# Output stores on ScalarE's queue, and another bounce tile for the sums of banks, in a fused attention and feed-forward kernel

## The chip, the cores and the metric

The kernel runs on one core of a Trainium2 chip. The metric is the device time of one execution in microseconds; of the kernel before there are three runs (609.57, 611.8 and 612.82 us, median 611.8) and one profiled execution (613.76 us, of which the profile covers a span of 611.9 us). The engines named below are TensorE (PE, with its weight loads as PEld), VectorE (DVE), ScalarE (ACT), GpSimd (POOL) and SyncE (SP), which does nothing but issue DMAs here. A queue name with a q at its end (SPq, ACTq) is the engine's instruction queue, where DMAs are issued.

## The reference

Decayed linear attention over blocks of 64 positions, then two matrix products with a leaky ReLU between:

```python
# q, k, v: (4, 8, 768, 64); lam: (8,);  w_in: (512, 2048); w_out: (2048, 512)
for b in range(nb):                       # 12 blocks of 64 positions
    intra = einsum('bhic,bhjc->bhij', qb, kb) * Dmask
    intra = einsum('bhij,bhjd->bhid', intra, vb)
    inter = einsum('bhid,bhde->bhie', qb * lam_pow, kv_state)
    out[:, :, sl] = intra + inter
    kv_state = lam_block * kv_state + einsum('bhsd,bhse->bhde', kb * rev_pow, vb)
x = out.transpose(0, 2, 1, 3).reshape(3072, 512)
h = x @ w_in
g = maximum(0.01 * h, h)
return g @ w_out                          # (3072, 512)
```

The products of the second part are done in three partial products each: an operand is split into a head `h` (ScalarE scales it by a little less than one into the reduced float32 form that TensorE takes), a rest `l` and a middle `m` (one VectorE pass each). A "conversion" below is this: one ScalarE instruction (L811, the head) and two VectorE passes (L814, L818), after which three matmuls per tile, over h, l and m, use the result.

## The kernel before

The 3072 tokens are six groups of 512, and the groups go in three pairs (`pr` 0 to 2, `gi` 0 and 1 within a pair). Until about 360 us the kernel does the attention and, woven into it, the first product with the leaky ReLU (`up`), whose results go to DRAM. After that it is in the stage that matters here, the product with `w_out`.

This stage is a list of units. `s(t, u)` is a product of a Strassen-like scheme (kinds 1 to 7, each in two halves u), `n(p, gi)` a plain product over one slice p of the 2048 columns. Each unit loads 512 KB from DRAM into a slot (`go`, L808, on SP), converts it (L811, L814, L818), and TensorE multiplies (L834). There are five slots used in turn, so a unit takes the slot that the unit five places earlier used, and its load waits until TensorE is done with that one. Kind 4 also loads a second operand into the tile `w32` (L825) and subtracts (L826) before it converts.

The results are summed in eight PSUM banks, in pairs named X, Z, Y and V. X and Z are the tiles `psc` and `po`, Y is `b10` and `b2`, V is `b11` and `pt`; the profile shows the three `b` banks alike as `b`. In the second and third pairs the order is: the last four units of the pair before (its `gi` = 1) mixed with `s(1,*)` and `s(6,*)`; a copy of X into Z and of Z into Y (`copy_banks`, L918, two ScalarE copies each); `s(5,*)`; Y += V (`add_banks`); `s(7,*)`; V += Z; then `s(3,0)`, `n(4,0)`, `s(2,0)`, `n(5,0)`, `s(3,1)`, `s(2,1)`, `n(6,0)`, `s(4,0)`, `s(4,1)`, `n(7,0)`. `add_banks` copies a bank to SBUF with ScalarE (L923) and adds it with VectorE (L924), bank by bank. The SBUF tile of this bounce is a piece of `gs`, which is also the tile `otile` that outputs are collected in.

With a group's last unit each finished bank is transposed from PSUM into `otile` by VectorE (`turn_out`, L902), and the output is stored from there (`store_out`, L911): four DMAs for each half m of a group's tokens, each from 32 partitions. A group's stores are so eight DMAs of 128 KB; the last group's are sixteen of 64 KB, since there two banks are stored as soon as they are ready, and the last bank is done in two halves of 256 columns.

What runs when is decided by a planner (`Plan`) when the program is built. Each operation is added with an engine, an estimated time, the keys it reads and writes, and a rank (place in the list plus an offset). `emit` simulates the engines: it always takes the operation that can start earliest, and among those that can start at the same time the one with the lowest rank. The order so found is fixed in each engine's program; at run time each engine goes through its own in order and waits on semaphores. "DMA" is SP. Conversions have the offset -LEAD (-8.0); copies and sums of banks, transposes and stores have -1.5. A store of four DMAs counts as one SP operation of 1.6 us.

Of the kernel before, what the change touches and what calls it, by code (L numbers as in the profile page):

```python
# [15 lines left out]
ALU = mybir.AluOpType  # L16
# [20 lines left out]
class Plan:  # L37
# [23 lines left out]
    def add(self, eng, us, fn, reads=(), writes=(), rank=0.0):  # L61

        n, deps = len(self.ops), set()
        for k in reads:
            w, r = self.last.setdefault(k, [None, []])
            if w is not None:
                deps.add(w)
            r.append(n)
        for k in writes:
            w, r = self.last.setdefault(k, [None, []])  # L70
            if w is not None:
                deps.add(w)
            deps.update(r)
            self.last[k] = [n, []]
        deps.discard(n)
        ways = {eng: us} if isinstance(eng, str) else dict(zip(eng, us))
        if self.slack:
            self.more[n] = self.slack
        if self.chain is not None:
            self.chains[self.chain].append(n)  # L80
        self.ops.append((ways, fn, deps, (self.rank + rank, n), set(writes)))
# [81 lines left out]
def kernel(  # L163
# [10 lines left out]
    nc = tc.nc  # L174
    P = 128
# [24 lines left out]
    LEAD = 8.0  # L200
# [3 lines left out]
    C4 = P // 4  # L204
# [8 lines left out]
    def sb(shape, name, dt=F32):  # L213
        return pool.tile(shape, dt, name=name, tag=name)
# [17 lines left out]
    w32 = sb([P, 2, d_model], "w32")  # L232
    w32f = w32.rearrange("p h n -> p (h n)")
    gst = sb([P, 2, 2, T], "gs")
    gs = [gst[:, i] for i in range(2)]
    WO = [dram.tile([P, 2 * d_model], F32, name=f"wo{p}", tag=f"wo{p}") for p in range(NP)]
    HT = T // 2
# [42 lines left out]
    add = plan.add  # L280
# [496 lines left out]
    acc = {"X": flat[:2], "Z": flat[2:], "Y": [b1[0], b2], "V": [b1[1], bank["pt"]]}  # L777
    ACC = {"X": ["X0", "X1"], "Z": ["Z0", "Z1"], "Y": ["b10", "b2"], "V": ["b11", "pt"]}
# [13 lines left out]
    def unit(src, keys, f=1, less=None):  # L792

        nonlocal n_ring
        j = slots[n_ring] if n_ring < len(slots) else RING[(n_ring - len(slots)) % NR]
        first, n_ring = j not in slots[:n_ring], n_ring + 1

        def wr(z):
            return [f"r{z}{j}"] + ([f"x{z}{j // 2}{cc}" for cc in range(GC)] if first and j < 4 else [])

        def m_slot():
            return ring[j][2].bitcast(F32)

        def g():
            return m_slot() if less is None else w32f

        def go():
            nc.sync.dma_start(out=m_slot().rearrange("p (f t) -> p f t", f=f), in_=src)  # L808

        def head():  # L810
            nc.scalar.activation(out=ring[j][0], in_=g(), func=AF.Copy, bias=0.0, scale=NEAR)  # L811

        def low():
            nc.vector.scalar_tensor_tensor(ring[j][1], g(), 1.0, ring[j][0].bitcast(F32), op0=ALU.mult, op1=ALU.subtract)  # L814

        def middle():
            h, l, m = ring[j]
            nc.vector.scalar_tensor_tensor(m, l.bitcast(F32), -S, h.bitcast(F32), op0=ALU.mult, op1=ALU.add)  # L818

        kg = [f"rm{j}"]  # L820
        add("DMA", 1.5, go, keys, wr("m"))
        if less is not None:
            x, k = less
            kg = ["w320", "w321"]
            add("DMA", 1.5, lambda: nc.sync.dma_start(out=w32f, in_=x), k, kg)  # L825
            add("DVE", 1.25, lambda: nc.vector.tensor_tensor(w32f, w32f, m_slot(), op=ALU.subtract), [f"rm{j}"], kg)  # L826
        add("ACT", 1.05, head, kg, wr("h"))
        add("DVE", 1.25, low, kg + [f"rh{j}"], wr("l"))
        add("DVE", 1.25, middle, [f"rh{j}", f"rl{j}"], [f"rm{j}"])
        return j  # L830

    def product(dst, j, col, lhs, first=False, n=T):
        for z in range(3):
            nc.tensor.matmul(dst, lhsT=lhs(z), rhs=ring[j][z][:, col:col + n], start=first and z == 0, stop=z == 2,  # L834
                             skip_group_check=True)
# [25 lines left out]
    def plain(pr, p, gi, lead, last=False, banks=None):  # L861

        g = 2 * pr + gi
        here = plan.rank
        plan.rank -= lead
        d = G[pr][p].rearrange("p (f h t) -> p f h t", f=2, h=2)[:, :, gi, :]
        j = unit(d, [x for x in plan.last if x[0] == "G" and x[1] in (str(2 * pr), str(2 * pr + 1)) and x[2:4] == f"{p}{gi}"], 2)
        plan.rank = here
        reads = [f"r{z}{j}" for z in "hlm"] + [f"w{z}{p}" for z in "hlm"]

        def go(fs, cs, lo=0, n=T):
            for f in fs:
                for c in cs:
                    d, i = BANKS[gi][c]
                    product(acc[d][i][:, lo:lo + n], j, f * T + lo,
                            lambda z, f=f, c=c: W[p][z][:, f * 2 * NQ + c * P:f * 2 * NQ + (c + 1) * P], first=pr == p == f == 0, n=n)

        if not last:
            add("PE", 0.227 * 24, lambda: go((0, 1), range(4)), reads, [ACC[d][i] for d, i in BANKS[gi]])
            return  # L880
        end = pr == NG // 2 - 1 and gi == 1
        for i, c in enumerate(banks):
            d, b = BANKS[gi][c]
            parts_ = 2 if end and i == 3 else 1
            for half in range(parts_):
                k = ACC[d][b] + (f"half{half}" if parts_ > 1 else "")
                n = T // parts_
                add("PE", 0.227 * 6 * (1.0 if parts_ == 1 else 0.53), lambda c=c, half=half, n=n: go((0, 1), (c,), half * n, n),
                    reads + ([ACC[d][b]] if parts_ > 1 else []), [k])
                turn_out(c, acc[d][b], [ACC[d][b], k], half * n, n)  # L890
                if i == 3 or end and i == 1:
                    cs = sorted(banks[:2] if end and i == 1 else banks[2:] if end else banks)
                    for m in ([half] if parts_ > 1 else range(2)):
                        store_out(pr, gi, m, cs)

    otile = gst.rearrange("p x f (b c j) -> p (x f b) c j", c=4, j=C4)

    def turn_out(c, b, keys, lo, n):
        nonlocal n_o
        n_o += 1  # L900
        o = otile[:, lo // C4:(lo + n) // C4, c, :]
        add("DVE", 0.1 + 0.6 * n / T, lambda: nc.vector.transpose(out=o, in_=b[:, lo:lo + n].rearrange("p (b i) -> p b i", i=C4)), keys,  # L902
            [f"o{c}{m}" for m in range(lo // HT, (lo + n) // HT)] + (["gs0", "gs1"] if n_o <= 4 else []), rank=-1.5)

    def store_out(pr, gi, m, cs):
        t0, n, w = (2 * pr + m) * T + gi * HT, HT // C4, len(cs) * C4

        def store():
            for a in range(4):
                c0 = a * P + cs[0] * C4  # L910
                nc.sync.dma_start(out=out[t0:t0 + HT, c0:c0 + w].rearrange("(b i) j -> i b j", i=C4),  # L911
                                  in_=otile[a * C4:(a + 1) * C4, m * n:(m + 1) * n, cs[0]:cs[-1] + 1, :].rearrange("i b c j -> i b (c j)"))

        add("DMA", 1.6, store, [f"o{c}{m}" for c in cs], [], rank=-1.5)

    def copy_banks(d, s):
        for i in range(2):
            add("ACT", 0.6, lambda i=i: nc.scalar.copy(acc[d][i], acc[s][i]), [ACC[s][i]], [ACC[d][i]], rank=-1.5)  # L918

    def add_banks(d, s):  # L920
        for i in range(2):
            y, key = gs[i][:, 0, :], [f"o{c}{i}" for c in range(4)]
            add("ACT", 0.6, lambda i=i, y=y: nc.scalar.copy(y, acc[s][i]), [ACC[s][i]], key, rank=-1.5)  # L923
            add("DVE", 0.72, lambda i=i, y=y: nc.vector.tensor_tensor(acc[d][i], acc[d][i], y, op=ALU.add), key, [ACC[d][i]], rank=-1.5)  # L924

    seq = [("a", 0), ("a", 1), ("a", 2), ("a", 3), ("wi", 1), ("b", 4), ("r", 4), ("up", 0, 1), ("wi", 0), ("r", 5),
# [26 lines left out]
    for pr in range(NG // 2):  # L953
# [11 lines left out]
        else:  # L965
            i = seq.index(("up", NG - 1, NP - 1))
# [73 lines left out]
```

## Time and profile before

| | |
|---|---|
| median of three runs | 611.8 us |
| profiled execution | 613.76 us |
| its span | 611.9 us |
| PE busy from 330 to 600 us, by stretches | all but 1.31 us |
| DVE / ACT busy over the span | 387.4 / 290.4 us |
| SP's queue | all DMAs of the kernel but one |
| output stores | 56 DMAs at L911, from 417.7 to 609.5 us |
| end of the last matmul, of the last store's landing, of the span | 603.5, 610.8, 611.9 us |

A row of a timeline has its start, its duration, the engine with the line of the kernel, the operation with out<-in tiles, and in brackets how long the engine was idle before and whom it waited for. A row of the chain of work has start, duration, and engine or DMA. The duration of a DMA row on SPq is the time that its issue took, not the transfer; "x8" there is a run of eight issues put together. Ends of matmuls are modelled, so distances between starts say more than their durations.

### The profile page before, as it was taken

The numbers are of one execution on the slowest core, as the hardware profiler recorded it, in microseconds if no ns is written. First come the engines' busy times: TensorE is split into PE (matmuls) and PEld (weight loads), VectorE is DVE, ScalarE is ACT, GpSimd is POOL, SyncE is SP. The second block draws the span as 40 slices with busy tenths as digits, with TensorE's granted clock in tenths as the row PEclk, the third lists the DMA queues.
The fourth block names the chain that finished last, engine by engine and source line by source line (L and its number), as shares of the span: only waits on it lengthen the run. The fifth ranks groups of instructions, "written<-read, shape, count | busy, mean of one in ns | idle before, by whom it ended". The sixth has DMA issues, their size and how long they took to land.

```text
span 611.9 us, 13190 instructions
## 1 busy us (share of the span) xinstructions
PE 591.6 (97%) x5340; PEld 488.7 (80%) x5340; DVE 387.4 (63%) x534; ACT 290.4 (47%) x458; POOL 85.9 (14%) x90
## 2 busy tenths in 40 slices
PE   7899999999989999999999999999999999999994
PEld 6688888888868877888888888888887888878883
DVE  4899764335436327426589849975688695778831
ACT  4678974445545545565576743432334223251300
POOL 1564422114214003203100000000000000000000
PEclk9899999999989999999999999999999999999998
DMA  9899776767889887999889735436465465474433
GB/s 217 212 261 254 228 193 145 171 151 204 196 218 264 216 220 218 235 235 260 265 256 333 233 113 197 170 123 185 139 182 195 152 193 176 155 225 140 158 80 69
DMA packets 190188, 119.88 MB, mean 196 GB/s; under 512 B 128944, under 2 KB 168112, under 8 KB 190128
## 3 DMA queue, kind: packets, MB, share of 16 engines
q1 hardware_dynamic: 189984, 119.05, 68.8%
q8 instruction: 42, 0.69, 0.5%
q14 instruction: 18, 0.15, 0.1%
q10 hardware_dynamic: 144, 0.00, 0.0%
HBM read 79.17 MB, written 39.85 MB: 194 GB/s over the span
## 4 chain that ended last, share of the span: by engine, by line
PE 84%; DMA 4%; SPq 4%; DVE 3%; ACT 2%; issue 1%; DVEq 0%; ACTq 0%
PE b L709 40%; PE b L834 11%; PE psc L834 11%; PE po L834 10%; PE po L321 4%; PE psc L321 4%; PE pt L834 4%; SPq L382 2%; SPq L911 2%; DMA att<-in_v_dram 1%; DMA raws<-in_moe_w_out_dram 1%; DVE xl L814 1%; PE pt L411 1%; DMA xm<-g 1%; DMA raws<-g 1%
## 5 line engine op out<-in xcount | busy, mean ns | idle before, releaser
L709 PE MATMUL b<-xm,wm 128*128 128x512 f32 (+2 forms) x392 | 103.9, 392 | 2.4 <-ACT b L727 2.4
L709 PE MATMUL b<-xh,wh 128*128 128x512 f32 (+2 forms) x392 | 103.5, 387 | 2.3 <-ACT gs L732 1.5
L709 PE MATMUL b<-xl,wl 128*128 128x512 f32 (+2 forms) x392 | 104.4, 390 | 0.0
L709 PEld LDWEIGHTS b<-xh,wh 128*128 128x128 f32 x392 | 72.8, 188 | 18.2 <-ACT gs L732 2.4
L811 ACT ACTIVATE xh<-xm 128x1024 fp32r<-128x1024 f32 x45 | 47.7, 1060 | 81.8 <-DMA xm<-g 50.9
L709 PEld LDWEIGHTS b<-xm,wm 128*128 128x128 f32 x392 | 71.4, 188 | 17.8 <-ACT b L727 3.2
L709 PEld LDWEIGHTS b<-xl,wl 128*128 128x128 f32 x392 | 72.8, 188 | 15.1 <-DVE wl L614 0.3
L732 ACT ACTIVATE gs<-b 128x512 f32<-128x512 f32 (+2 forms) x97 | 56.9, 591 | 50.6 <-PE b L709 37.4
L727 ACT ACTIVATE b<-b 128x512 f32<-128x512 f32 (+2 forms) x97 | 56.1, 581 | 52.2 <-PE b L709 52.0
L814 DVE SCALAR_TENSOR_TENSOR xl<-xm,xh 128x1024 fp32r<-128x1024 f32 x45 | 54.8, 1217 | 28.3 <-ACT xh L811 22.1
L818 DVE SCALAR_TENSOR_TENSOR xm<-xl,xh 128x1024 fp32r<-128x1024 f32 x48 | 58.7, 1225 | 3.5
L470 POOL TENSOR_TENSOR att<-att 128x256 f32<-128x256 f32 x40 | 34.1, 853 | 53.9 <-DVE att L467 53.9
L602 DVE TENSOR_SCALAR w<-w 128x512 int32<-128x512 int32 x32 | 17.6, 550 | 36.9 <-ACT w L596 36.8
L431 POOL TENSOR_TENSOR att<-att 128x512 f32<-128x512 f32 (+1 forms) x20 | 25.2, 1261 | 102.0 <-DVE att L391 53.9
L460 DVE TENSOR_TENSOR att<-psc,att 128x512 f32<-128x512 f32 x24 | 16.5, 689 | 31.3 <-PE psc L321 31.2
L321 PEld LDWEIGHTS po<-att 64*64 64x64 f32 x1472 | 28.3, 140 | 9.1 <-issue 6.0
L321 PE MATMUL po<-att 64*64 64x64 f32 x1472 | 34.1, 228 | 0.6 <-ACT att L499 0.3
L427 POOL TENSOR_TENSOR att<-att 128x512 f32<-128x512 f32 (+1 forms) x23 | 26.7, 1161 | 53.7 <-DMA att<-in_k_dram 35.9
L603 DVE CUSTOM_DVE_ANT_0 w<-w,lows 128x1024 uint16<-128x1024 uint16 x32 | 26.3, 821 | 12.6 <-ACT lows L600 11.4
L834 PE MATMUL b<-xl,wl 128*128 128x512 f32 (+1 forms) x86 | 33.0, 384 | 0.0
L834 PE MATMUL b<-xm,wm 128*128 128x512 f32 (+1 forms) x86 | 33.0, 384 | 0.0
L834 PE MATMUL b<-xh,wh 128*128 128x512 f32 (+1 forms) x86 | 33.0, 384 | 0.0
(149 smaller groups left out, 1011.2 us busy)
## 6 DMA issues: line engine op xcount, KB each, us to landing
g<-gs SPq DMA_DIRECT2D x31, 512.0 KB, 4.1
xm<-g SPq DMA_DIRECT2D x25, 512.0 KB, 4.7
xm<-b SPq DMA_DIRECT2D x23, 512.0 KB, 3.8
raws<-in_moe_w_in_dram SPq DMA_DIRECT2D x16, 512.0 KB, 5.5
raws<-in_moe_w_out_dram SPq DMA_DIRECT2D x16, 512.0 KB, 5.0
b<-gs SPq DMA_DIRECT2D x16, 512.0 KB, 3.7
att<-in_k_dram SPq DMA_DIRECT2D x48, 128.0 KB, 4.0
att<-in_v_dram SPq DMA_DIRECT2D x24, 256.0 KB, 4.5
```

The lines of the kernel that those rows point to most:

```text
L321: nc.tensor.matmul(dst[HALF[cols]], lhsT=lhsT[HALF[rows]], rhs=rhs[HALF[rows]], start=start, stop=True, skip_group_check=True)
L427: lambda e="POOL": ENG[e].tensor_tensor(kr[nr], kr[nr], _bc(pow_k, 3, D)[nr], op=ALU.mult), ["fk"], [f"k{i}"])
L431: add(eng, us, lambda: e.tensor_tensor(o, x, _bc(pow_q, 2, 2)[:, :, m, :], op=ALU.mult), ["fq", dep], [f"qsT{i}"])
L470: add("POOL", 0.7, lambda new=new, j=j: nc.gpsimd.tensor_tensor(state[(j + 1) % 4], new, _bc(lam_c, 2, D), op=ALU.mult), [f"st{j % 4}", "f ...
L603: add("DVE", 1.0, lambda: nc.vector.tensor_tensor(d, d, low, op=ALU.add), [kl], [key])
L709: nc.tensor.matmul(dst, lhsT=w[z][:, kk * 2 * P + f * P:kk * 2 * P + (f + 1) * P], rhs=x[z][:, kk, toks], start=start and kk == 0, stop=kk ...
L727: add("ACT", ns, lambda b=b: nc.scalar.activation(out=b, in_=b, func=AF.Copy, bias=0.0, scale=S + 1.0), [], [kb], rank=-1.5)
L732: add("ACT", t, lambda o=o, x=s_: nc.scalar.activation(out=o, in_=x, func=AF.Prelu, bias=0.0, scale=(1.0 + 1.0 / S) / (WS * U), alpha=0.01 ...
L811: nc.scalar.activation(out=ring[j][0], in_=g(), func=AF.Copy, bias=0.0, scale=NEAR)
L814: nc.vector.scalar_tensor_tensor(ring[j][1], g(), 1.0, ring[j][0].bitcast(F32), op0=ALU.mult, op1=ALU.subtract)
L818: nc.vector.scalar_tensor_tensor(m, l.bitcast(F32), -S, h.bitcast(F32), op0=ALU.mult, op1=ALU.add)
L834: nc.tensor.matmul(dst, lhsT=lhs(z), rhs=ring[j][z][:, col:col + n], start=first and z == 0, stop=z == 2, skip_group_check=True)
```

## The change

Three things are changed. The stores are added to the plan one DMA at a time, at 0.5 us: those of all groups but the last go to ScalarE, with rank offset 6.0 in place of -1.5; those of the last group go to ScalarE and SP in turns, with -1.5. The bounce of `add_banks` lies in the tile `w32`, with its keys, instead of in `gs` with the keys of the output tile. Copies and sums of banks have the rank offset -LEAD, like conversions.

```diff
-                        store_out(pr, gi, m, cs)
+                        store_out(pr, gi, m, cs, end)
...
-    def store_out(pr, gi, m, cs):
+    def store_out(pr, gi, m, cs, last):
         t0, n, w = (2 * pr + m) * T + gi * HT, HT // C4, len(cs) * C4
 
-        def store():
-            for a in range(4):
-                c0 = a * P + cs[0] * C4
-                nc.sync.dma_start(out=out[t0:t0 + HT, c0:c0 + w].rearrange("(b i) j -> i b j", i=C4),
-                                  in_=otile[a * C4:(a + 1) * C4, m * n:(m + 1) * n, cs[0]:cs[-1] + 1, :].rearrange("i b c j -> i b (c j)"))
-
-        add("DMA", 1.6, store, [f"o{c}{m}" for c in cs], [], rank=-1.5)
+        def store(a, q):
+            c0 = a * P + cs[0] * C4
+            q.dma_start(out=out[t0:t0 + HT, c0:c0 + w].rearrange("(b i) j -> i b j", i=C4),
+                        in_=otile[a * C4:(a + 1) * C4, m * n:(m + 1) * n, cs[0]:cs[-1] + 1, :].rearrange("i b c j -> i b (c j)"))
+
+        for a in range(4):
+            e = "DMA" if last and (a + m) % 2 else "ACT"
+            add(e, 0.5, lambda a=a, e=e: store(a, nc.scalar if e == "ACT" else nc.sync), [f"o{c}{m}" for c in cs], [], rank=-1.5 if last else 6.0)
 
     def copy_banks(d, s):
         for i in range(2):
-            add("ACT", 0.6, lambda i=i: nc.scalar.copy(acc[d][i], acc[s][i]), [ACC[s][i]], [ACC[d][i]], rank=-1.5)
+            add("ACT", 0.6, lambda i=i: nc.scalar.copy(acc[d][i], acc[s][i]), [ACC[s][i]], [ACC[d][i]], rank=-LEAD)
 
     def add_banks(d, s):
         for i in range(2):
-            y, key = gs[i][:, 0, :], [f"o{c}{i}" for c in range(4)]
-            add("ACT", 0.6, lambda i=i, y=y: nc.scalar.copy(y, acc[s][i]), [ACC[s][i]], key, rank=-1.5)
-            add("DVE", 0.72, lambda i=i, y=y: nc.vector.tensor_tensor(acc[d][i], acc[d][i], y, op=ALU.add), key, [ACC[d][i]], rank=-1.5)
+            y, key = w32[:, i, :], [f"w32{i}"]
+            add("ACT", 0.6, lambda i=i, y=y: nc.scalar.copy(y, acc[s][i]), [ACC[s][i]], key, rank=-LEAD)
+            add("DVE", 0.72, lambda i=i, y=y: nc.vector.tensor_tensor(acc[d][i], acc[d][i], y, op=ALU.add), key, [ACC[d][i]], rank=-LEAD)
```

## The prediction

> **What bounds the kernel now.** I read the shares first, then the matmuls of the last stage by stretches, then the two places where they pause, then the tail.
>
> ```profile
> PE 591.6 (97%) x5340; PEld 488.7 (80%) x5340; DVE 387.4 (63%) x534; ACT 290.4 (47%) x458; POOL 85.9 (14%) x90
> 410.00:599.00 189.00, 187.69 (x826) 154.53 (x826) 1.00 0.52 162
> 600.00:612.00 12.00, 3.53 (x22) 2.98 (x20) 0.75 0.41 87
> ```
>
> TensorE is busy for 97% of the span. All output stores lie after 410 us. From there to 599 us (second row: window, length, PE busy, weight loads, clock, DMA share, GB/s) the matmuls lack 1.3 us out of 189, so an edit to this stage can win almost nothing except in those pauses and in the last 8.4 us, where PE has stopped (third row). The pauses:
>
> ```profile
> 462.65 0.39 PE L834 MATMUL psc<-xl,wl 128*128 128x512 f32 x1
> 463.52 0.50 PE L834 MATMUL psc<-xm,wm 128*128 128x512 f32 x1 [0.48 <-DVE xm L818]
> 545.17 0.50 PE L834 MATMUL psc<-raws,wl 128*128 128x512 f32 x1
> 546.50 0.50 PE L834 MATMUL psc<-raws,wm 128*128 128x512 f32 x1 [0.83 <-DVE raws L818]
> ```
>
> A matmul takes 187.69 / 826 = 0.227 us in this stage. Here the steps between starts are 0.87 and 1.33 us: 0.64 and 1.10 us too long, 1.74 us together. The chain of work that ended last says why:
>
> ```profile
> 454.80 0.48 SPq L911
> 455.39 4.35 DMA xm<-g
> 459.82 1.07 ACT xh L811
> 460.91 1.24 DVE xl L814
> 462.24 1.24 DVE xm L818
> ...
> 535.12 1.82 SPq L911
> 538.57 4.14 DMA raws<-g
> ```
>
> Both pauses are the first product of `n(4,0)`, the first plain product of the second and of the third pair of groups. Its data were loaded late because SP was issuing eight output stores, as SP's queue shows, and the buffer had been free for some time:
>
> ```profile
> 450.31 4.97 SPq L911 DMA_DIRECT2D out_dram<-gs  x8
> 455.39 0.52 SPq L808 DMA_DIRECT2D xm<-g  x1
> 532.76 5.71 SPq L911 DMA_DIRECT2D out_dram<-gs  x8
> 538.57 0.52 SPq L808 DMA_DIRECT2D raws<-g  x1
> 601.52 7.96 SPq L911 DMA_DIRECT2D out_dram<-gs  x16
> 451.31 0.39 PE L834 MATMUL pt<-xm,wm 128*128 128x512 f32 x1
> 533.76 0.39 PE L834 MATMUL pt<-raws,wm 128*128 128x512 f32 x1
> ```
>
> With five buffers in turn, `n(4,0)` takes the one that `s(5,0)` used; its last matmuls are the last two rows, starting at 451.31 and 533.76, so by the ends of these rows it is free at 451.70 and 534.15. The loads went out at 455.39 and 538.57: 3.7 and 4.4 us later, with the stores between. The fifth row is the tail, sixteen stores one after another on SP.
>
> **The change part by part.**
>
> *Stores of all groups but the last, SP to ScalarE.* 40 of the 56 DMAs of L911 leave SP. SP's next loads can go when their buffer is free: 451.7 instead of 455.4, and 534.15 instead of 538.6. They now share the DMA engines with the stores, so I don't take the landings of 4.35 and 4.14 us but the longest of this stretch:
>
> ```profile
> DMA to landing us min/median/max: 3.3/3.8/5.4
> ```
>
> 451.7 + 5.4 = 457.1; then head 1.07 and two DVE passes of 1.24, with 0.1 of gaps: 460.8. The third matmul is due at 462.88. In the next pair 534.15 + 5.4 + 3.65 = 543.2, due at 545.4 less the 0.64 won before, 544.76. Both pauses go, by 2.1 and 1.6 us. What is late next is then that same unit, through DVE (below). Gain 1.74 us; bounds 0 (the loads win nothing) and 2.1 (the three matmuls that show 0.50 us instead of 0.39 beside a pause become short too, 0.33 us more).
>
> *What it costs ScalarE.* ScalarE's program in the first of the two places:
>
> ```profile
> 450.32 0.57 ACT L918 COPY b<-po 128x512 f32<-128x512 f32 x1 [0.73 <-DVE gs L902]
> 450.80 1.06 ACT L811 ACTIVATE xh<-xm 128x1024 fp32r<-128x1024 f32 x1
> 452.97 1.06 ACT L811 ACTIVATE xh<-xm 128x1024 fp32r<-128x1024 f32 x1 [1.11 <-DMA xm<-b]
> 455.29 0.59 ACT L923 COPY gs<-b 128x512 f32<-128x512 f32 x1 [1.25 <-DMA out_dram<-gs]
> 457.21 0.59 ACT L923 COPY gs<-pt 128x512 f32<-128x512 f32 x1 [1.33 <-PE po L834]
> 459.82 1.06 ACT L811 ACTIVATE xh<-xm 128x1024 fp32r<-128x1024 f32 x1 [2.02 <-DMA xm<-g]
> ...
> L911 SPq DMA_DIRECT2D out_dram<-gs x56: 316/468/1822, 417.7 to 609.0; - x56
> ```
>
> A store waits only for transposes that are over when it becomes ready; but as the queue is in order, heads and copies stand behind it while it issues. The head of `n(4,0)` must start by 462.88 - 1.07 - 2.48 - 0.1 = 459.2. From 450.3 that is 8.9 us, less a copy (0.57), two heads (2.12) and two bounces (1.18): 5.0 us are free for eight stores, 0.63 us each. At the tail's pace, 7.96 / 16 = 0.50 us with the gap between issues, they need 4.0 (the median issue of the last row is 0.468). So they are hidden, at 0 us, by ScalarE's waits for loads. Bounds: 0, and the eight stores at 0.71 us each (5.71 / 8): 0.7 us late. Rank 6.0 lets heads and copies that are ready in the plan go first, so I take 0. In the other three groups PE pauses nowhere near the stores (1.3 us is all that is idle up to 599), and what covers them is again ScalarE's waiting for loads; 0.
>
> *Bounce in w32 instead of gs.* The bounce no longer waits for the old stores to have read `gs` (the 1.25 us before 455.29). No pause of PE hung on it, so this wins 0. In return the w32 load of `s(4,0)`, fetched far ahead until now, waits on SP for the second sum, with the loads of `s(2,1)` and later queued behind it:
>
> ```profile
> L825 SPq DMA_DIRECT2D w<-b x4: 320/330/872, 399.3 to 563.6; - x4
> 473.24 0.69 DVE L924 TENSOR_TENSOR b<-b,gs 128x512 f32<-128x512 f32 x1
> 471.59 0.32 SPq L808 DMA_DIRECT2D xm<-b  x1
> 476.91 1.22 DVE L826 TENSOR_TENSOR w<-w,xm 128x1024 f32<-128x1024 f32 x1
> ```
>
> The load that went at 399.3 now goes after the sums, at about 463 us by their new rank, and lands, again at the longest 5.4 us, at 468.4. The subtraction that reads it ran at 476.91, because its other operand was only asked for at 471.59. Cover of 3 us or more; cost 0. Even with the sum left at 473.24 it would be about 479, and DVE's work after that would shift by 2 us: the upper bound.
>
> *Sums ahead of conversions.* The two additions into V ran from 473.24, behind conversions; with rank -8 they run as soon as the copies are there, near 461. That puts 2 x 0.69 = 1.4 us in front of the conversions of `n(4,0)` if both are ready together: 460.8 + 1.4 = 462.2 against 462.88, and 543.2 + 1.4 = 544.6 against 544.76. Just covered, so 0; if landing or stores take a little longer it costs up to 1.4 us per place, but that can't exceed the pause that is there now by much. This is the thin part of the sum.
>
> *The tail.* Here the durations lie open:
>
> ```profile
> 600.78 0.72 DVE L902 STREAM_TRANSPOSE gs<-pt 128x512 f32<-128x512 f32 x1 [0.65 <-PE pt L834]
> 603.57 0.78 DVE L902 STREAM_TRANSPOSE gs<-b 128x256 f32<-128x256 f32 x2 [0.71 <-PE b L834]
> 604.00:605.00 1.00, 0.00 (x0) 0.00 (x0) 0.35 (x2) 0.00 (x0) 0.00 (x0) 1.00 0.59 128
> L1035 SPq EVENT_SEMAPHORE  x8: 17/28/28, 610.8 to 611.9; - x8
> out_dram<-gs SPq DMA_DIRECT2D x16, 64.0 KB, 1.8
> ```
>
> The data of the last eight stores are there at 604.0 and 604.35, but SP, at 0.50 us per store, is with the first eight until 605.5 and starts the last at 609.0; 1.8 us later (last row: bytes of one store, median us to landing) it has landed, 610.8, and 1.1 us of closing follow. With two queues in turn: four each from 601.52, free at 603.5; two each at 604.0 (to 605.0); two each at 605.0, the last starting at 605.5. That is 3.5 us earlier. The DMA engines move 128 GB/s at a share of 0.59, so at full share about 217 GB/s (an estimate from this row): the last eight, 8 x 64 KB = 0.52 MB, need 2.4 us from about 604.6, which ends at 607.0 and some queueing. I charge 0.3 us for it: gain 3.2 us. Bounds: 3.5, and 0 if the two queues can't issue at once. The nearest row for that is the opening, the only place where both issue together:
>
> ```profile
> 0.73 0.43 ACTq L268 DMA_DIRECT2D att<-in_lam_dram  x1
> 0.74 0.46 SPq L346 DMA_DIRECT2D att<-in_k_dram  x1
> ```
>
> They overlap whole and neither is longer than usual, so I take the value for parallel issue. Against it stands the Trainium skill, page "Perfetto Trace Analysis", section "DMA Instruction — HWDGE (DVE, Sync)": descriptors are made in one block that the sequencers share, each locking it for itself while it generates. By that rule alone the tail would win nothing and the sum would be 1.74 us; the overlapped pair does not agree with a lock over the whole issue.
>
> **Sum.** 1.74 + 3.2 = 4.9 us. The profiled execution took 613.76 us (span 611.9 and 1.9 around it), 2.0 above the median of the runs shown, 611.8. So 608.8 in such an execution, and 611.8 - 4.9 = 606.9 as a median.
>
> **Rivals.**
>
> *The queues take turns.* ScalarE's and SP's issues serialise. For it: issues in the crowded stretch were already stretched to 1.82 us on one queue; against it: the opening pair. Loads still get in between stores, so the pauses go: 611.8 - 1.74 = 610.1. The page named above speaks for this one.
>
> *The pauses stay, in another form.* The sums in front on DVE and the stores on ScalarE make `n(4,0)` as late as SP did. For it: the 0.2 us of slack worked out above; against it: the load gains 3.7 and 4.4 us. Only the tail wins: 611.8 - 3.2 = 608.6.
>
> *Slower: ScalarE is held by its stores.* Where the DMA engines are full, an issue waits; on SP that only delays loads, on ScalarE it stops heads and bounces at 450 and 533 us. Free are 0.63 us per store. At 1.2 us each (between the mean of 0.71 and the longest of 1.82), 8 x 0.57 = 4.6 us late, in two places 9.1; less the tail 3.2: 611.8 + 5.9 = 617.7. It decides from (3.1 + 3.2) / 16 + 0.63 = 1.0 us per store. Against it: the mean was 0.62 and 0.71 there, and heads that are ready go first.
>
> **How the numbers follow.** Forecast 0.55 (its own range 605.9 to 608.3: tail 2.8 to 3.5, pauses 0.7 to 2.1, a few tenths of spread between runs), queues in turn 0.14, pauses stay 0.18, ScalarE held 0.09, others 0.04. The range runs from 605.6 to 610.4: it reaches down to both gains at their upper bound (611.8 - 5.6 = 606.2) with some spread, up past the case of queues in turn, and leaves out the held ScalarE and the rest. Half a per cent, about what can be told from no change, is 3.06 us: under 608.74 is faster. Faster: 0.95 of the forecast, half of "pauses stay", 0.01 of the others: 0.62. Slower: 0.09 + 0.01. The rest, 0.28, is the same.
>
> **What would show it.** Right: no store in SP's queue until the last set; `n(4,0)` loaded within half a microsecond of its buffer's release; no idle step above 0.3 us in its matmuls; the last sixteen stores on two queues within 4.2 us, and a span that ends about 5 us after the last matmul instead of 8.4. Wrong: stores on ScalarE of a microsecond and more with heads waiting behind them; issues on the two queues that never overlap or double in length; sums standing between the head and the passes of `n(4,0)`; a new idle step of PE at `s(4,0)` after a w32 load that came late.

## The result, and the profile after

The changed kernel takes 607.94 us as the median of 13 runs (606.0 to 610.33), the kernel before, in 13 runs beside them, 612.43 us (609.57 to 616.61). The ratio is 0.9925, with a 95% interval of 0.9908 to 0.9943: 4.5 us faster. The forecast was 606.9 us and a gain of 4.9 us. The profiled execution took 606.94 us, its span is 605.2 us.

The spans of the two profiled executions differ by 6.7 us, more than the medians. About 2 us of that lie ahead of the first output, where nothing was changed; that part of the kernel moves by as much from run to run (its end, the first L902, lies between 410.6 and 414.6 us in the fourteen traces of this document). So the comparison is best made from a mark inside the trace. The timelines have one on each side of the stage: the first transpose of an output (L902) and the last matmul. First the kernel before, then the changed one:

```profile
413.66 1.31 DVE L902 STREAM_TRANSPOSE gs<-psc 128x512 f32<-128x512 f32 x2 [0.53 <-PE psc L834]
603.25 0.28 PE L834 MATMUL b<-xm,wm 128*128 128x256 f32 x1
```

```profile
411.62 1.31 DVE L902 STREAM_TRANSPOSE gs<-psc 128x512 f32<-128x512 f32 x2 [0.23 <-PE psc L834]
599.05 0.28 PE L834 MATMUL b<-xm,wm 128*128 128x256 f32 x1
```

From the start of the first row to the end of the second it is 603.53 - 413.66 = 189.87 us before and 599.33 - 411.62 = 187.71 us after: 2.16 us gained in the stage. From the end of the last matmul to the end of the span it is 8.37 us before and 605.2 - 599.33 = 5.87 us after: 2.50 us gained in the tail. The sum, 4.7 us, is the gain of the medians within their spread.

**The stage.** The stretch that lacked 1.31 us of matmuls, in the view by stretches of the changed kernel (L834 alone; window, length, PE busy, weight loads, clock, DMA share, GB/s):

```profile
410.00:599.00 189.00, 189.00 (x840) 156.69 (x840) 1.00 0.54 165
```

TensorE no longer pauses. The timeline around the two first products of `n(4,0)` says why; SPq and ACTq rows are issues of DMAs:

```profile
448.29 0.90 ACTq L910 DMA_DIRECT2D out_dram<-gs  x2
448.76 1.06 ACT L811 ACTIVATE xh<-xm 128x1024 fp32r<-128x1024 f32 x1
449.22 1.45 ACTq L910 DMA_DIRECT2D out_dram<-gs  x2
449.28 0.39 PE L834 MATMUL pt<-xm,wm 128*128 128x512 f32 x1
449.70 0.52 SPq L808 DMA_DIRECT2D xm<-g  x1
454.92 0.32 ACTq L910 DMA_DIRECT2D out_dram<-gs  x1
455.29 1.06 ACT L811 ACTIVATE xh<-xm 128x1024 fp32r<-128x1024 f32 x1 [2.20 <-DMA xm<-g]
455.32 1.67 ACTq L910 DMA_DIRECT2D out_dram<-gs  x3
457.71 1.23 DVE L818 SCALAR_TENSOR_TENSOR xm<-xl,xh 128x1024 fp32r<-128x1024 f32 x1
458.86 0.69 DVE L925 TENSOR_TENSOR b<-b,w 128x512 f32<-128x512 f32 x1
460.84 0.39 PE L834 MATMUL psc<-xm,wm 128*128 128x512 f32 x1
460.99 0.38 SPq L825 DMA_DIRECT2D w<-b  x1
...
530.88 0.39 PE L834 MATMUL pt<-raws,wm 128*128 128x512 f32 x1
531.30 0.52 SPq L808 DMA_DIRECT2D raws<-g  x1
```

The load of `n(4,0)` goes out 0.03 us after its buffer comes free (449.28 + 0.39 = 449.67, and 531.27 in the next pair), instead of 3.7 and 4.4 us later. Its data are converted at 457.71 + 1.23 = 458.94 and the third matmul, which needs them, starts at 460.84: 1.9 us of slack. The stores lie in two parts, four ahead of ScalarE's wait for that load and four at its end. That they stop in between has a reason that the prediction did not have. In the trace all DMAs of the program use eight semaphores in turn, and an issue waits until the DMA that used its semaphore before has landed; more than eight are never under way. The fifth store has the semaphore of the load of `n(4,0)`. The load landed at 454.90, the store went at 454.92, and the head, behind it in ScalarE's order, at 455.29: it waited for its load and then 0.3 us for one store.

**The tail.** The same timeline, then the last issues grouped by line (name, count, shortest/median/longest in ns, first and last start), the closing line in the same form, and one microsecond of the tail by stretches:

```profile
597.33 4.43 SPq L910 DMA_DIRECT2D out_dram<-gs  x8
597.33 4.60 ACTq L910 DMA_DIRECT2D out_dram<-gs  x8
```

```profile
L910 SPq DMA_DIRECT2D out_dram<-gs x8: 316/394/474, 597.3 to 601.4; - x8
L910 ACTq DMA_DIRECT2D out_dram<-gs x8: 323/420/497, 597.3 to 601.6; - x8
...
DMA to landing us min/median/max: 2.0/2.5/2.8
```

```profile
L1036 SPq EVENT_SEMAPHORE  x8: 17/28/155, 603.9 to 605.1; - x8
```

```profile
601.00:602.00 1.00, 0.00 (x0) 0.00 (x0) 0.00 (x0) 0.00 (x0) 0.00 (x0) 0.99 0.98 199
```

The two queues issue side by side, at no more per DMA than one queue alone. The last store starts 2.3 us after the last matmul's end (601.6 to 599.33) where it was 5.5 (609.0 to 603.53). But where the DMA engines stood at a share of 0.59 while one queue issued, they are now full, at about 200 GB/s, and the median store takes 2.5 us to land instead of 1.8. The closing begins at 603.9, when SyncE's last store has landed; ScalarE's last, issued at 601.6, lands at 604.1, and the longest wait of the closing (155 ns) is the one for it.

### The profile page after: what moved, and what is told of

Same layout as the page of the kernel before. It is cut to its first block, busy times and chain, and to the rows that moved or that the text cites. A ratio compares the mean times of both kernels' runs of the same rounds, so it can differ in the third digit from the quotient of the medians.

```text
span 605.2 us, 13193 instructions
## 1 busy us (share of the span) xinstructions
PE 589.9 (97%) x5340; PEld 487.4 (81%) x5340; DVE 387.6 (64%) x534; ACT 290.0 (48%) x458; POOL 86.2 (14%) x90
## 3 DMA queue, kind: packets, MB, share of 16 engines
q10 hardware_dynamic: 13200, 5.77, 3.8%
## 4 chain that ended last, share of the span: by engine, by line
PE 89%; DMA 5%; DVE 1%; ACT 1%; SPq 1%; issue 0%; POOL 0%; DVEq 0%; ACTq 0%
PE b L709 38%; PE b L834 13%; PE po L834 13%; PE psc L834 11%; PE pt L834 4%; PE psc L321 4%; PE po L321 4%; DMA b<-gs 2%; DMA raws<-in_moe_w_out_dram 1%; SPq L382 1%; DMA att<-in_v_dram 1%; PE pt L411 1%; DMA att<-in_k_dram 1%; PE po L411 0%; PE b L274 0%
## 5 line engine op out<-in xcount | busy, mean ns | idle before, releaser
L603 DVE CUSTOM_DVE_ANT_0 w<-w,lows 128x1024 uint16<-128x1024 uint16 x32 | 27.8, 868 | 12.4 <-ACT lows L600 11.2
L834 PE MATMUL b<-xl,wl 128*128 128x512 f32 (+1 forms) x86 | 33.0, 384 | 0.0
L834 PE MATMUL b<-xm,wm 128*128 128x512 f32 (+1 forms) x86 | 33.0, 384 | 0.0
L834 PE MATMUL b<-xh,wh 128*128 128x512 f32 (+1 forms) x86 | 33.0, 384 | 0.0
```

The lines of the kernel that those rows point to most:

```text
L603: add("DVE", 1.0, lambda: nc.vector.tensor_tensor(d, d, low, op=ALU.add), [kl], [key])
```

## The experiments

The line numbers of stores and sums shift by a few lines between kernels. "Stage" is the time from the first L902 to the end of the last matmul as above (before 189.87 us, changed kernel 187.71), "tail" what follows to the end of the span (8.37 and 5.87). These two are from one profiled execution each; times are medians, ratios are to the kernel before on the same chip.

| run | stage, us | tail, us | ratio (95%) |
|---|---|---|---|
| changed kernel | 187.71 | 5.87 | 0.9925 (0.9908 to 0.9943) |
| tail_only | 189.93 | 5.61 | 0.9965 (0.9951 to 0.9980) |
| body_only | 206.98 | 8.47 | 1.0306 (1.0285 to 1.0328) |
| bounce_only | 193.52 | 8.36 | 1.0053 (1.0020 to 1.0087) |
| stores_only | 206.60 | 5.69 | 1.0267 (1.0243 to 1.0291) |
| gs_new_ranks | 202.33 | 5.69 | 1.0143 (1.0093 to 1.0194) |
| w32_old_ranks | 198.13 | 5.77 | 1.0099 (1.0067 to 1.0132) |
| sp_late | 187.71 | 5.60 | 0.9923 (0.9899 to 0.9947) |
| twice_on_act | 187.71 | 5.67 | 607.92 us, one run, to 612.78 |
| rank_early | 200.55 | 5.64 | 622.32 us, one run, to 612.78 |
| last_all_act | 187.71 | 8.53 | 609.03 us, one run, to 612.78 |
| two_banks_first | 187.72 | 5.71 | 0.9934 (0.9906 to 0.9962) |
| token_halves | 187.95 | 5.23 | 0.9917 (0.9887 to 0.9947) |

**One part at a time: tail_only, body_only, bounce_only.** The first is the kernel before with only the last set in turns. The diff is against the changed kernel and is cut; tile and ranks are put back in it too:

```diff
+        if not last:
+            add("DMA", 1.6, lambda: [store(a, nc.sync) for a in range(4)], [f"o{c}{m}" for c in cs], [], rank=-1.5)
+            return
         for a in range(4):
             e = "DMA" if last and (a + m) % 2 else "ACT"
...
```

> The kernel before with one part of the change: the last group's sixteen stores go out on ScalarE and SyncE in turns, all else as before. My theory (the tail is won by two queues issuing at once until the transfers bound it; the pauses are another matter): both pauses at the first product of n(4,0) stay, about 0.6 and 1.1 us too long; from the end of the last matmul to the end of the span 5.9 us instead of 8.4; 2.5 us less than the kernel before. Rival (the gain is one of order in the middle of the stage, and the tail only looks shorter): within 0.5 us of the kernel before.

It measured 608.63 us to 610.74: 2.1 us gained. Its tail is that of the changed kernel, its stage that of the kernel before, and the waits of PE between 410 and 599 us (for whom: us, times, longest) all lie in the third pair, at both passes of the unit `n(4,0)`:

```profile
PE psc L834 <- DVE raws L818: 0.8, 1, 0.8
PE psc L834 <- DVE raws L814: 0.4, 1, 0.4
```

By the steps between starts the matmuls there are 0.59 and 1.10 us late. In the second pair the third matmul is 0.26 us late (461.14 to 461.63), too little for this list. The place is the old one, but the sizes, expected at 0.6 and 1.1, move from run to run.

The second run is the kernel before with only the other stores moved to ScalarE, at rank 6.0; the bounce stays in `gs` and the sums at -1.5 (again a cut diff against the changed kernel):

```diff
+        if last:
+            add("DMA", 1.6, lambda: [store(a, nc.sync) for a in range(4)], [f"o{c}{m}" for c in cs], [], rank=-1.5)
+            return
         for a in range(4):
...
+            add(e, 0.5, lambda a=a, e=e: store(a, nc.scalar if e == "ACT" else nc.sync), [f"o{c}{m}" for c in cs], [], rank=-1.5 if last else 6.0)
```

> The kernel before with one part: stores of all groups but the last on ScalarE with rank 6.0, the last group's sixteen on SyncE as before, bounce in gs and old ranks as before. My theory so far (the pauses come only from stores ahead of loads on SyncE): pauses at n(4,0) gone, tail 8.4 us, 1.7 to 2.1 us less. Rival (the bounce in gs now waits for stores that ScalarE issues late): the second copy of Y += V can't start until stores issued at about 456 us have been read, 3 us later; s(3,0) then waits 2 to 2.5 us in each of two places, and the kernel takes 2 to 3 us more than before although n(4,0) is on time.

It measured 629.06 us, 18.3 us slower than before. My theory had no loss at all; the rival had the cause and the place (`s(3,0)`, in two places), but 2 to 3 us for what costs 18. The waits of PE:

```profile
PE b L834 <- DVE b L928: 15.4, 2, 8.4
```

L928 is here the addition of `add_banks`. What it waits for is shown with stores_only, where the same happens.

The third run is the kernel before with only the new bounce tile and the new ranks (the additions and `copy_banks` change theirs likewise):

```diff
-            y, key = gs[i][:, 0, :], [f"o{c}{i}" for c in range(4)]
+            y, key = w32[:, i, :], [f"w32{i}"]
...
-            add("ACT", 0.6, lambda i=i, y=y: nc.scalar.copy(y, acc[s][i]), [ACC[s][i]], key, rank=-1.5)
+            add("ACT", 0.6, lambda i=i, y=y: nc.scalar.copy(y, acc[s][i]), [ACC[s][i]], key, rank=-LEAD)
```

> The kernel before with one part: bounce in w32 and rank -LEAD for copies and sums, all stores on SyncE as before. My theory: n(4,0) is still loaded late; in the program the two sums into V now stand between its two VectorE passes, 1.3 us, so each pause grows by about 1.2 us: 2 us or so slower than before. Rival (order and bounce are what removed the pauses): pauses gone, 1.7 to 2.1 us less.

It measured 614.98 us to 610.74, 0.5% slower. Waits of PE, then VectorE's timeline:

```profile
PE psc L834 <- DVE raws L818: 1.8, 1, 1.8
PE psc L834 <- DVE xm L818: 1.4, 1, 1.4
```

```profile
458.52 1.23 DVE L814 SCALAR_TENSOR_TENSOR xl<-xm,xh 128x1024 fp32r<-128x1024 f32 x1 [3.02 <-ACT xh L811]
459.66 0.70 DVE L924 TENSOR_TENSOR b<-b,w 128x512 f32<-128x512 f32 x1
460.26 0.69 DVE L924 TENSOR_TENSOR pt<-pt,w 128x512 f32<-128x512 f32 x1
460.86 1.22 DVE L818 SCALAR_TENSOR_TENSOR xm<-xl,xh 128x1024 fp32r<-128x1024 f32 x1
```

The two sums stand between the two passes of `n(4,0)`, whose load is still late behind SP's stores, and lengthen its pauses to 3.7 us together (steps between matmul starts of 1.83 and 2.33 us, where 0.227 is usual; the list above shows the idle part). This is the cost that the prediction set an upper bound to (1.4 us per place). In the changed kernel both passes of `n(4,0)` come before the first sum at 458.86. So of the three parts alone one wins 0.35%, one loses 0.5% and one 3.1%, and together they win 0.75%: they can't be added up.

**stores_only.** The changed kernel with bounce and ranks put back (the diff of bounce_only, reversed).

> The changed kernel without its second and third parts: all stores as changed, bounce in gs and ranks as before. If the stores alone make the gain: as the changed kernel, 4.5 us less than before. If the bounce in gs waits for stores issued late on ScalarE: no pause at n(4,0), the tail of the changed kernel (5.9 us), but a wait of 2 to 2.5 us at s(3,0) in two places, so about the time of the kernel before.

It measured 626.3 us, 15.6 us slower than before. ScalarE's timeline, and two rows from the chain of work:

```profile
454.06 0.59 ACT L924 COPY gs<-b 128x512 f32<-128x512 f32 x1 [3.07 <-DMA out_dram<-gs]
454.09 1.04 ACTq L910 DMA_DIRECT2D out_dram<-gs  x2
...
455.19 1.04 ACTq L910 DMA_DIRECT2D out_dram<-gs  x2
459.78 0.59 ACT L924 COPY gs<-pt 128x512 f32<-128x512 f32 x1 [3.55 <-DMA out_dram<-gs]
460.26 1.06 ACT L811 ACTIVATE xh<-xm 128x1024 fp32r<-128x1024 f32 x1
```

```profile
448.73 5.19 DMA out_dram<-gs
...
455.69 4.02 DMA out_dram<-gs
```

The bounce copy overwrites the piece of `gs` that the old stores read, so it waits until they have landed, 5.2 and 4.0 us after their issue beside the early loads. The stores of the second half of the tokens (454.09, 455.19) go out only behind the first copy, so the two waits come one after the other. ScalarE is in order, so the head at 460.26 stands too, and then the sum into Y, which `s(3,0)` needs: PE pauses 7 to 8 us in each of the two pairs. It was not the time of issuing that held ScalarE, but a copy queued on it that waits for a landing.

A pause so long costs more than itself. By stretches of the same kernel, over the pause and behind it (the clock is the third number from the right):

```profile
458.00:464.00 6.00, 0.00 (x0) 0.00 (x0) 3.36 (x4) 2.97 (x4) 0.00 (x0) 0.74 0.37 126
464.00:468.00 4.00, 3.42 (x9) 2.71 (x10) 3.90 (x4) 1.54 (x2) 0.00 (x0) 0.54 0.00 0
```

The granted clock falls to 0.50 at about 460.9, inside the pause, and comes back at about 467.7, some 3 us after the matmuls resume: nine matmuls take from 464.58 to 468.18, 3.6 us, where 9 x 0.227 = 2.0 would do.

**Tile and rank apart: w32_old_ranks and gs_new_ranks.** With the stores on ScalarE, one run has the new tile with the old ranks, the other the old tile with the new ranks.

> The changed kernel with copies and sums back at rank -1.5; the bounce stays in w32. Stores on ScalarE with the bounce in gs cost 15.6 us; this asks which of the other two parts takes that away. My theory: the tile alone, since what was waited for was the stores' reading of gs (landings of 5.19 and 4.02 us in the chain). Then no pause at s(3,0), and within 1 us of the changed kernel. Rival (the copies must also rank ahead of heads): a pause of 1 us or more at s(3,0) or n(4,0), 2 us or more slower than the changed kernel.

> The changed kernel with the bounce back in gs; copies and sums keep rank -LEAD. My theory: a rank can't shorten a wait for a transfer: s(3,0) pauses 6 to 8 us in each of two places, 12 to 16 us slower than the changed kernel. Rival (the rank gets the copies in front of the stores): within 3 us of the changed kernel; the order of the keys makes this impossible for the second copy, whose piece of gs the stores have still to read.

The first measured 618.77 us to 612.58, the second 621.96. My theory that the tile alone is what protects falls, that with `gs` the kernel stays slow holds. w32_old_ranks, waits of PE, then VectorE and ScalarE:

```profile
PE b L834 <- DVE b L925: 6.8, 2, 3.7
```

```profile
452.70 0.59 ACT L924 COPY w<-pt 128x512 f32<-128x512 f32 x1
...
459.99 1.23 DVE L818 SCALAR_TENSOR_TENSOR xm<-xl,xh 128x1024 fp32r<-128x1024 f32 x1
461.13 0.69 DVE L925 TENSOR_TENSOR b<-b,w 128x512 f32<-128x512 f32 x1
```

The copy is done at 453.3, but its sum runs only at 461.13, behind the conversions of two later units, whose loads now arrive early. In the changed kernel both sums into Y are over by 454.7. gs_new_ranks, ScalarE:

```profile
463.24 0.59 ACT L924 COPY gs<-pt 128x512 f32<-128x512 f32 x1 [4.64 <-DMA out_dram<-gs]
```

The new rank does not get this copy past the stores: the four that read its piece of `gs` stand ahead of it. The last of them went at 458.17, after waiting for a load that had its semaphore, and landed 5.0 us later, at 463.17. Stores on ScalarE so need both: the old tile costs 14.6 us of stage, the old ranks 10.4, both together 18.9 (202.33, 198.13 and 206.60 less 187.71).

**Queue or order: sp_late, twice_on_act, rank_early.** sp_late is the changed kernel with the stores of all groups but the last on SP again, one by one and with rank 6.0:

```diff
-            e = "DMA" if last and (a + m) % 2 else "ACT"
+            e = "DMA" if not last or (a + m) % 2 else "ACT"
```

> The changed kernel, but the stores of all groups but the last stay on SyncE, as single DMAs of 0.5 us with rank 6.0; the last set in turns as in the changed kernel. In its program the loads stand between the stores (two stores, a load, three stores, a load, two, a load, one). My theory: what made the pauses was that eight stores stood as one block ahead of the load; the queue itself doesn't matter: n(4,0) is loaded at most 2 us after its buffer is free, no pause, tail 5.9 us, within 1 us of the changed kernel. Rival (loads need a queue without stores): pauses of 0.5 us or more come back and it is 1 to 2 us slower than the changed kernel.

It measured 608.56 us to 612.58, as the changed kernel, without a pause. SP's queue:

```profile
450.24 0.89 SPq L910 DMA_DIRECT2D out_dram<-gs  x2
451.66 0.52 SPq L808 DMA_DIRECT2D xm<-g  x1
452.23 1.77 SPq L910 DMA_DIRECT2D out_dram<-gs  x3
```

The load slips in between two stores. What had made the pauses was not that SP carried the stores, but that eight went out as a block ahead of the load.

twice_on_act cuts each of those stores in two, so ScalarE issues 16 per group instead of 8.

```diff
+        k = n if last else n // 2
         for a in range(4):
+            for lo in range(0, n, k):
...
+                add(e, 0.5, lambda a=a, e=e, lo=lo: store(a, nc.scalar if e == "ACT" else nc.sync, lo, k), [f"o{c}{m}" for c in cs], [], rank=-1.5 if last else 6.0)
```

> The changed kernel with each store of all groups but the last cut into two DMAs of half the rows, so 16 instead of 8 issues per group on ScalarE. The prediction's rival held that ScalarE, with 5.0 us free, is held by its stores from 1.0 us per store of 128 KB on; two halves take about that. Rival: pauses of 2 to 3 us come back at n(4,0). My theory now: with rank 6.0 heads and copies go first, so the stores only stretch (to about 465 us) and nobody waits for them but the next group's transposes, 40 us later: no pause of PE, tail 5.6 to 5.9 us.

One run took 607.92 us, with no pause. The issues of the first pair's last group stretch out behind ready heads and copies, and four of them go just when the load that had their semaphore before has landed (454.9, 461.1, 467.9 and 469.3):

```profile
L910 ACTq DMA_DIRECT2D out_dram<-gs x16: 322/392/652, 449.4 to 469.3; - x16
```

rank_early gives the stores the rank -20 in place of 6.0, so that they come first.

> The changed kernel with the stores of all groups but the last at rank -20 instead of 6.0: in ScalarE's program eight stores then stand as one block ahead of the second copy, both bounces and two heads. My theory (the rank is what keeps ScalarE's stores harmless): heads due at 448.8 and 451 us wait until about 455, and s(7,0) or s(7,1) pauses 2 to 4 us in each of two places. Rival (ScalarE is half idle, so the order does not matter): no pause.

One run took 622.32 us, 9.5 us over the median before. ScalarE's timeline, and a row from the chain of work:

```profile
450.97 7.95 ACTq L910 DMA_DIRECT2D out_dram<-gs  x8
458.96 0.57 ACT L919 COPY b<-po 128x512 f32<-128x512 f32 x1 [8.72 <-DMA out_dram<-gs]
```

```profile
452.38 6.19 DMA xm<-g
```

The copy of Z into Y that is queued behind the block stands for 8.72 us, and PE, which writes Z next, pauses 4.5 us here and 3.3 us in the third pair. The block's 7.95 us are not all issuing: seven stores go out from 450.97 to 455.20, 0.60 us each, and the eighth goes only at 458.60. It has the semaphore of the load in the last row, that of `n(4,0)`, which lands at 458.57. The third pair shows the same, with 2.3 us before the eighth store instead of 3.4. So the rank is what keeps ScalarE free, not the small number of stores: it puts ready work ahead both of the issues and of this wait. How much the block would cost without the shared semaphore was not tried.

**The tail: last_all_act, two_banks_first, token_halves.** In last_all_act the last sixteen go to ScalarE alone (`e = "ACT"`).

> The changed kernel with the last group's sixteen stores all on ScalarE. My theory (one queue issues at 0.50 us per store, whichever it is): from the end of the last matmul to the end of the span 8.4 us, as with all on SyncE. Rival (ScalarE's queue is the quicker one): 6 us or less.

Timeline, and a stretch of the tail:

```profile
596.76 8.02 ACTq L910 DMA_DIRECT2D out_dram<-gs  x16
```

```profile
600.00:601.00 1.00, 0.00 (x0) 0.00 (x0) 0.00 (x0) 0.00 (x0) 0.00 (x0) 1.00 0.61 130
```

The tail is 8.53 us, as with SP alone, at 130 GB/s where that had 128. So the gain lies in two queues issuing at once, and not in which one does.

two_banks_first tests what holds the rest of the tail. It moves work of `n(6,1)` so that the first two banks end 2.72 us earlier and the first eight stores are out of the way of the last eight.

```diff
+        if not last and end and p == NP - 2:
+            add("PE", 0.227 * 12, lambda: go((0, 1), (2, 3)), reads, [ACC[d][i] for d, i in BANKS[gi][2:]])
+            held.append(lambda: add("PE", 0.227 * 12, lambda: go((0, 1), (0, 1)), reads, [ACC[d][i] for d, i in BANKS[gi][:2]]))
+            return
...
+            if end and i == 1:
+                held.pop()()
```

> The changed kernel with the last two units in another order: n(6,1) does the banks of V, then n(7,1) does them, then n(6,1) the banks of Y, so V is finished 12 matmuls (2.72 us) earlier and its eight stores are through when the last eight begin. My theory (the tail of the changed kernel is bound by transfers, share 0.98 to 1.04 for four us, where sixteen stores overlap): the last landing falls from 2.5 to about 1.9 us, and the last store starts 0.5 us sooner after the last matmul; tail 5.0 us or a little less instead of 5.9. Rival (the tail is bound by issuing): the last eight still start at the same distance, 5.9 us stays.

It won nothing: 608.61 us, tail 5.71. The DMA engines were idle before the last eight stores, and these alone fill them:

```profile
605.00:606.00 1.00, 0.00 (x0) 0.00 (x0) 0.00 (x0) 0.00 (x0) 0.00 (x0) 1.00 1.01 198
```

The theory that the sixteen stores are in each other's way falls: eight on two queues already ask for all that the engines give.

token_halves does the last unit by halves of the tokens instead of pairs of banks: eight stores of 128 KB in place of sixteen of 64 KB, each with runs of 512 bytes in DRAM in place of 256.

```diff
+        if end:
+            n = T // 2
+            for half in range(2):
+                for c in range(4):
...
+                    turn_out(c, acc[d][b], [ACC[d][b], k], half * n, n)
+                store_out(pr, gi, half, [0, 1, 2, 3], end)
+            return
```

> The changed kernel with the last unit done by halves of the tokens (256 columns of all four banks, then the other 256) instead of by banks, so that the last set is eight stores of 128 KB with runs of 512 bytes instead of sixteen of 64 KB with 256. My theory (after two_banks_first, where the last eight stores alone took as long: the tail is bound by the bytes of the last half megabyte at about 200 GB/s): larger runs move faster (274 GB/s at full share at 420 us in the kernel before) and need half the issues, so tail 4.8 to 5.1 us instead of 5.7 to 5.9, less 0.25 us for 24 more narrow matmuls; 0.6 us in all, too little for the time to tell from the changed kernel. Rival (the landing is what lasts, not the bytes): tail 5.6 us or more.

```profile
604.00:605.00 1.00, 0.00 (x0) 0.00 (x0) 0.00 (x0) 0.00 (x0) 0.00 (x0) 0.50 0.97 255
```

At full share the engines now write 255 GB/s, and the tail is 5.23 us, little more than the 4.8 to 5.1 expected. The time, 607.9 us to 612.78, can't be told from that of the changed kernel: 0.6 us are within the interval. No version that ran is clearly better than the changed kernel.

## Why the prediction was right

**The loads (forecast 1.74 us).** Right. Load to converted data took 458.94 - 449.70 = 9.2 us (forecast 9.1), and the slack at the third matmul was 1.9 us (forecast 2.1, without the sums). The stage gained 2.16 us, at the upper bound of 2.1. sp_late shows that the step was named too narrowly: the block had to go, not the queue.

**ScalarE's time (forecast 0).** Right in the number. The eight stores took 0.90 + 1.45 + 0.32 + 1.67 = 4.3 us of the 5.0 that were free (forecast 4.0), and the head waited for its load and 0.3 us for a store, which the slack covered. Cut in two they cost nothing either. The rival of a held ScalarE names a real danger: without the rank it happened, though not through the pace of 1.0 us per store that the rival asked for. Seven stores took 0.60 us each, and the eighth waited 3.4 us for a load's landing. The prediction gave the rank half a sentence; rank_early makes it a condition.

**Bounce in `w32` "wins 0", sums ahead "0".** The sum came out, the reasoning fails. Both were priced against the kernel before, where the bounce's wait of 1.25 us held up nobody. They should have been priced against the kernel with the stores moved: there the old tile costs 14.6 us and the old ranks 10.4. What I called the thin part, sums in front of `n(4,0)`, does occur (bounce_only, 3.7 us of pauses), but only where the load is late; with the early load the conversions come first. The later load of `w32` cost nothing, as said: it went at 460.99 (forecast about 463) and no pause of PE followed.

**The tail (forecast 3.2 us).** The mechanism was right, the term was mis-sized: 2.5 us. Two queues issue at once, but the sixteen stores took 4.6 us, not the 4.2 named as a sign. The last store started 3.2 us earlier relative to the last matmul (5.5 to 2.3), not 3.5; and it then landed in 604.1 - 601.6 = 2.5 us instead of 1.8, 0.7 longer where I had charged 0.3. The closing behind it took 1.1 us in both kernels. 3.2 - 0.7 = 2.5. The full DMA engines, which the prediction put at 217 GB/s, were seen at about 200, and token_halves shows that the form of the transfers changes this rate.

The start that came 0.3 us late is the work of the eight semaphores again: each of the last four went within 0.1 us of the landing of the store eight places before it (600.86, 601.02, 601.42 and 601.58; issued at 600.92, 601.10, 601.43 and 601.61), though the transposes were over at 600.15. In two_banks_first, where the last eight wait for no earlier store, the last one starts 1.95 us after the last matmul, as counted; its tail is no shorter for it, so the full DMA engines bound the end either way.

The changed kernel's tail is also the longest of its kind: seven other traces with the same last stores have 5.60 to 5.77 us, so 0.1 to 0.3 us of what is missing may be spread. The sum came out better than its terms, for the loads won 0.4 us more than forecast and the tail 0.7 less.

**Rivals.** *Queues take turns* fell: sixteen issues in 4.6 us against 8.0. The rule of the Trainium skill that spoke for it ("Perfetto Trace Analysis", section "DMA Instruction — HWDGE (DVE, Sync)", one sequencer at a time holds the shared descriptor block) is not what these rows show for SP and ACT: 0.394 and 0.420 us per issue side by side, 0.466 (SP) and 0.470 (ACT, last_all_act) alone. A lock over a part of the issue is not ruled out by them. *Pauses stay* fell for the change as a whole; sums in front on VectorE came true in bounce_only, where the load is late.

## What to carry to other kernels

Price each part of a change against the kernel with the other parts in it, not only against the one before: a part that wins nothing may be what keeps another from losing 15 us. Where stores move to an engine that also computes, look for every instruction there that overwrites what the stores read, for the order in which the issues stand in that engine's queue, and for what an issue itself can wait for, here any DMA that had its semaphore before. When transfers are issued one at a time and the DMA engines stand at a share of 0.6, a second queue wins until they are full; after that only the form of the transfer is left.

## What the runs showed of the hardware

- Two queues issue DMAs at the same time without lengthening each other (16 in 4.6 us against 8.0 on one). The Trainium skill says ("DMA: Bandwidth & Descriptors", section "Issuing engines are not separate DMA queues") that all DMAs share the same 16 engines and that a second issuing engine saves only the issuing time, usually a small part. The first half agrees with the full share at 200 GB/s here. This tail is no such usual case: issuing was the bound, and its saving was 2.5 of 8.4 us.
- ScalarE goes on with an instruction while its queue issues DMAs: the head at 448.76, 1.06 us long, runs beside issues at 448.29 and 449.22. What suffers is the instruction queued behind.
- One issue took 0.32 to 0.50 us in the changed kernel's tail, also with the DMA engines full, 0.32 to 0.90 in the block of rank_early beside loads, and once 1.82 in the kernel before. What lengthens it was not tried; a full share alone does not.
- The queues do not run freely ahead: with eight semaphores in turn for all DMAs of this program, a store can stand for the landing of a load on another queue (3.4 us in rank_early). This is read from the traces; no run had another number of semaphores.
- With each pause of TensorE of 3 to 8 us in these runs the granted clock went to 0.50 (a mean of 0.54 in the stretch shown), and matmuls ran slowly for some 3 to 6 us, which added 1.5 to 2.9 us to the pause. In bounce_only this already followed the pause of 1.8 us, but not the one of 1.4, which is why its stage lost more than its pauses show.
- Stores of 128 KB with runs of 512 bytes went at 255 GB/s with the engines full, those of 64 KB with 256 bytes at 198 and 199. Size and runs were changed together.
- Left open: what moves the part of the kernel ahead of the first output by some microseconds from run to run, and how short the tail could become.
